# Memory layers in a periodic order with three of four chain images transposed by DMA

## The chip, the cores and the metric

The kernel runs on one core of one Trainium2 chip. A core has TensorE (matmuls into PSUM, a small memory of eight banks), VectorE, ScalarE and GpSimd for elementwise work, SyncE (SP), which here only issues DMAs, and 16 DMA engines. Every engine takes its instructions in the order written, and engines wait for one another through semaphores. The metric is the device time of one execution in microseconds. Three runs of the kernel before gave a median of 2031.8 us (2031.22 to 2032.16).

## The reference

Input x is 2048 rows of 512 numbers in bf16. Four layers follow one another, each adding its result to x: a memory layer A, a linear attention layer B, A again, B again. Each works on the layer-normalised x.

```python
for s in range(n_seg):                    # 64 segments of 32 rows
    h = concatenate([mem, xs])            # 8 memory rows + 32 rows of x
    q, k, v = h @ Wq, h @ Wk, h @ Wv      # 32 heads of 128
    scores = q @ k.T * scale              # 40 x 40, causal among the rows of x;
                                          # every query sees all 8 memory rows
    o = softmax(scores) @ v @ Wo
    mem = o[:8]                           # goes into the next segment
    outs.append(o[8:])
```

The 8 memory rows of a segment come out of the segment before, so layer A is a recurrence of 64 steps. Layer B is, for 32 heads of 16, o = phi(q) (phi(k)^T v) / (phi(q) sum phi(k)), then a projection; it has no recurrence over segments.

## The kernel before

A step of the recurrence uses a block of 32 rows: the 8 memory rows and 24 of the segment's 32 rows of x. The remaining 8 rows of each of four segments do not fit; they form a block of 32 "left" rows, one for each group of four segments (`left_block`, line 671), worked on ahead of time.

**Chain images.** `project` (line 633) multiplies a block by half of the heads of a weight matrix: 16 matmuls of 512 columns, each on one of four column tiles of the array, so that 32 rows of output stand at four places of PSUM. For queries and keys the result is copied to SBUF as an image of 128x512 and must then be transposed for the scores. `transposed` (line 645) does this on TensorE for the four images of a segment (queries and keys, each in two halves of the heads): four transposes into PSUM (L655) and a copy. `turned` (line 662) does it for the left block by one DMA transpose from SBUF to SBUF (L668), issued on SP. Values need no transpose.

**Memory attention** (line 708), for each half: a mask matmul (L717), scores of the memory's queries against left keys and own keys (L725), an exponential, sums (L737), a reciprocal by logarithm and exponential (L740, L742), products with the values (L750, L751), a multiplication (L754). Then comes the output projection (L823, column tiles) and `next_mem` (L842), which selects the 8 new memory rows and puts them into the next block: the recurrence closes there.

**x attention** (line 759) treats the other queries, off the recurrence: its scores (L774) are 32 matmuls on column tiles, for each head over 24 own queries and 8 left queries side by side. For this the left queries are copied behind the own ones into `qT` first, which is 40 wide for this purpose (line 768). Sums (L786, L787), products (L807, L808) and, a segment later, the output projection follow; `residual` (L857) adds the rows to x.

**Order.** `_Prog.schedule` (line 125) writes the order of all engines by a list scheduler over a table of costs. Among the instructions that are ready on an engine it picks the one with the highest priority, which is the length of the longest chain behind it (its "tail"). On TensorE it prefers an instruction of the same mode (column tiles, "col", or full array, "full") if its priority is within `MODE_SLACK`, and counts `PE_SWITCH` = 0.1 us for a change of mode. PSUM tiles take one of the eight banks when their first instruction is picked. Instructions marked urgent, those of the recurrence, may take one of the last free banks.

## Time and profile before

| | us |
|---|---|
| median of three runs | 2031.8 |
| profiled execution | 2032.45 |
| its span, first to last instruction | 2030.7 |
| TensorE busy | 1946.7 (96%) |
| ScalarE busy | 1274.8 (63%) |
| VectorE busy | 1015.3 (50%) |
| DMA transposes | 128, 2.5 from issue to landing |

In a row of the profile stand the line of the kernel, the engine (PE is TensorE's matmuls, PEld its weight loads, DVE VectorE, ACT ScalarE, SPq SP's queue), the operation, what is written and read, the shape and how many. In a group of instructions the busy time, the mean duration of one in ns and the idle time ahead of them follow; in a view in order of time the start and duration stand first. Durations of matmuls overlap, since they are pipelined: what a matmul costs is the time until the next one starts.

### The profile page before, as it was taken

What the parts mean: (1) busy time and instruction counts of PE and PEld (TensorE: products, weight loads), DVE (VectorE), ACT (ScalarE), POOL (GpSimd) and SP (SyncE); (2) the same over time, 40 slices, a digit from 0 to 9 for tenths busy, and PEclk for the clock granted to TensorE, in tenths of its full rate; (3) what the DMA queues carried; (4) which work ended last, traced back from release to release, by engine and by line L of the source; (5) the groups of instructions that cost most, each with busy time, mean ns of one, the idle gap of its engine ahead of it and who ended that gap; (6) DMA issues with size and microseconds to landing.
All of it is one profiled execution on the core that took longest, in us unless ns stands there. A gap on an engine that the chain in (4) does not pass through costs nothing.

```text
span 2030.7 us, 81374 instructions
## 1 busy us (share of the span) xinstructions
PE 1946.7 (96%) x37214; PEld 1150.5 (57%) x37214; DVE 1015.3 (50%) x3068; ACT 1274.8 (63%) x3203; POOL 23.6 (1%) x88
## 2 busy tenths in 40 slices
PE   2999999999999999997989999999999999999988
PEld 0555556555555555554645555555556555555555
DVE  0544444544444444445865444444444444444578
ACT  1666666666666666665646666666666666666654
POOL 3000000000000000000010000000000000000000
PEclk8999999999999999998999999999999999999989
DMA  9100000000000000001010000000000000000011
GB/s 362 34 10 13 10 13 11 12 10 13 13 11 13 13 14 10 13 8 43 1 15 16 8 13 11 13 13 13 10 13 13 10 11 13 13 10 13 5 42 43
DMA packets 82184, 47.17 MB, mean 23 GB/s; under 512 B 70056, under 2 KB 79280, under 8 KB 80304
## 3 DMA queue, kind: packets, MB, share of 16 engines
q1 hardware_dynamic: 81840, 41.97, 9.0%
q8 instruction: 291, 4.77, 1.0%
q14 instruction: 53, 0.43, 0.1%
HBM read 23.08 MB, written 2.10 MB: 12 GB/s over the span
## 4 chain that ended last, share of the span: by engine, by line
PE 93%; DMA 2%; DVE 2%; ACT 1%; issue 0%; SPq 0%; DVEq 0%
PE pb L639 43%; PE pb L823 15%; PE pb L655 6%; PE pb L842 3%; PE pb L807 3%; PE pb L944 3%; PE pb L725 3%; PE pb L857 2%; PE pb L737 2%; DMA Wv_sb<-in_A_Wv_dram 2%; PE pb L717 2%; PE pb L774 2%; PE pb L1011 1%; PE pb L937 1%; PE pb L750 1%; PE pb L751 1%
## 5 line engine op out<-in xcount | busy, mean ns | idle before, releaser
L516 ACT ACTIVATE arena_sb<-pb 128x512 bf16<-128x512 f32 (+6 forms) x1535 | 796.0, 523 | 421.9 <-PE pb L639 275.7
L639 PE MATMUL pb<-Wk_sb,arena_sb 128*32 128x512 bf16 x5120 | 353.3, 384 | 0.8 <-ACT arena_sb L516 0.8
L823 PE MATMUL pb<-Wo_sb,arena_sb 128*32 128x512 bf16 x5184 | 337.1, 384 | 8.7 <-DVE arena_sb L754 8.3
L639 PE MATMUL pb<-Wq_sb,arena_sb 128*32 128x512 bf16 x5120 | 344.4, 383 | 0.5 <-ACT arena_sb L516 0.5
L517 DVE COPY arena_sb<-pb 128x512 bf16<-128x512 bf16 (+2 forms) x474 | 178.5, 405 | 311.1 <-PE pb L655 307.4
L639 PE MATMUL pb<-Wv_sb,arena_sb 128*32 128x512 bf16 x5120 | 323.5, 380 | 0.5 <-DMA Wv_sb<-in_A_Wv_dram 0.5
L795 DVE TENSOR_TENSOR arena_sb<-arena_sb 32x256 bf16<-32x256 bf16 x512 | 213.3, 417 | 162.5 <-ACT arena_sb L791 150.6
L517 DVE CAST arena_sb<-pb 128x128 bf16<-128x128 f32 (+3 forms) x357 | 132.7, 375 | 179.6 <-PE pb L808 64.0
L639 PEld LDWEIGHTS pb<-Wk_sb,arena_sb 128*32 128x32 bf16 x5120 | 132.9, 97 | 126.9 <-issue 5.1
L639 PEld LDWEIGHTS pb<-Wq_sb,arena_sb 128*32 128x32 bf16 x5120 | 127.2, 97 | 130.7 <-ACT arena_sb L516 7.6
L639 PEld LDWEIGHTS pb<-Wv_sb,arena_sb 128*32 128x32 bf16 x5120 | 130.6, 96 | 121.7 <-DMA Wv_sb<-in_A_Wv_dram 0.6
L823 PEld LDWEIGHTS pb<-Wo_sb,arena_sb 128*32 128x32 bf16 x5184 | 122.1, 96 | 120.8 <-issue 11.3
L516 ACT ACTIVATE outW_sb<-pb 128x256 fp32r<-128x256 f32 x155 | 59.3, 382 | 184.8 <-PE pb L823 184.7
L655 PE MATMUL pb<-id_sb,arena_sb 128*128 128x128 bf16 x2048 | 157.3, 219 | 0.0
L655 PEld LDWEIGHTS pb<-id_sb,arena_sb 128*128 128x128 bf16 x2048 | 122.6, 97 | 55.4 <-ACT arena_sb L516 54.4
L807 PE MATMUL pb<-arena_sb 128*128 128x128 bf16 x1024 | 125.0, 217 | 4.1 <-DVE arena_sb L797 4.1
L797 DVE TENSOR_TENSOR arena_sb<-arena_sb 32x64 bf16<-32x64 bf16 x512 | 111.1, 217 | 15.8
L808 PE MATMUL pb<-arena_sb 128*128 128x32 bf16 x1024 | 114.3, 178 | 0.0
L732 ACT ACTIVATE arena_sb<-pb 128x256 bf16<-128x256 f32 x256 | 92.4, 383 | 32.9 <-PE pb L725 27.2
L842 PEld LDWEIGHTS pb<-selm_sb,outW_sb 128*128 128x128 f32 x504 | 75.1, 188 | 64.8 <-ACT arena_sb L778 23.8
L725 PE MATMUL pb<-arena_sb 128*128 128x32 bf16 x2048 | 102.8, 177 | 0.0
L517 DVE CAST outW_sb<-pb 128x256 fp32r<-128x256 f32 x105 | 44.5, 424 | 106.5 <-ACT outW_sb L516 103.4
(106 smaller groups left out, 2314.0 us busy)
## 6 DMA issues: line engine op xcount, KB each, us to landing
Wk_sb<-in_A_Wk_dram SPq DMA_DIRECT2D x1, 4096.0 KB, 12.6
Wq_sb<-in_A_Wq_dram SPq DMA_DIRECT2D x1, 4096.0 KB, 22.7
Wv_sb<-in_A_Wv_dram SPq DMA_DIRECT2D x1, 4096.0 KB, 31.9
Wo_sb<-in_A_Wo_dram SPq DMA_DIRECT2D x1, 4096.0 KB, 43.8
arena_sb<-in_B_wqkv_dram SPq DMA_DIRECT2D x2, 1536.0 KB, 6.3
arena_sb<-arena_sb SPq DMA_TRANSPOSE x128, 2.5
out_dram<-x_sb SPq DMA_DIRECT2D x16, 128.0 KB, 1.7
x_sb<-in_A_x_dram SPq DMA_DIRECT2D x1, 1920.0 KB, 9.3
```

The source lines that it names most:

```text
L516: return e.activation(o() if callable(o) else o, i() if callable(i) else i, ACTF.Copy)
L517: return e.tensor_copy(o() if callable(o) else o, i() if callable(i) else i)
L639: r = pe.matmul(tl.f32()[32 * j:32 * j + 32, 0:512], blk[:, c, :], W[:, c, o:o + 512], start=(c == 0), stop=(c == 3), tile_position=(0, 32 ...
L655: r = pe.transpose(tt.bf16()[:, 128 * i:128 * i + 128], img[:, k, 128 * i:128 * i + 128], id_sb[:, :])
L725: r = pe.matmul(tl.f32()[:, o:o + 32], kk[:, hh, :, :].rearrange("p j x -> p (j x)"), qT[:, r2, hh, :, 0:8], start=False, stop=True, skip_ ...
L732: add("act", lambda a: a.activation(Pm[:, k, :, :].rearrange("p a q -> p (a q)"), tl.f32()[:, 0:256], ACTF.Exp, scale=SCALE), c_act(256), ...
L795: add("dve", lambda v, q=q, j=j: v.tensor_tensor(Pbx[q, :, j, 0:32], Px[q, :, :], Rx[q, :, :], ALU.mult), c_dve(256), reads=["Px", "Rx"], ...
L797: add("dve", lambda v, q=q, j=j: v.tensor_tensor(Pbx[q, :, j, 32:40], PLL[q, g2, :, gl], Rx[q, :, 24:32], ALU.mult), c_dve(64), reads=[("P ...
L807: pe.matmul(o, vimg[:, r2, e], Pbx[:, hh, :, 0:32], start=True, stop=False)
L808: return pe.matmul(o[:, :, 24:32], vleft[:, g2, e], Pbx[:, hh, :, 32:40], start=False, stop=True)
L823: r = pe.matmul(tl.f32()[32 * j:32 * j + 32, :], oT[:, 4 * hh + j, :], Wo_sb[:, 8 * j + hh, :], start=(hh == 0), stop=(hh == 7), tile_posi ...
L842: r = pe.matmul(tl.f32()[:, 8 * c:8 * c + 8], outW[:, s % 3, 128 * c:128 * c + 128], selm_sb[:, :], start=True, stop=True)
```

## The change

The change has three parts.

First, `transposed` and `turned` become one function with a switch. Of a segment's four images, both halves of the queries and the first half of the keys now go through a DMA transpose on SP; the second half of the keys stays on TensorE. The scheduler's figures for a DMA transpose change from 0.1 us of issue and 3.0 us of latency to 1.25 and 1.25.

Second, the left queries are no longer copied into `qT`, which is 32 wide now. The x scores do, for each head, one matmul over the 24 own queries and one over the 8 left queries where they lie.

Third, the order. Each instruction of the memory layers gets a place: the segment (step), a kind of work and a number in it. Its priority is -(step x PERIOD + offset), from a table of offsets for each kind, in place of its tail. `MODE_SLACK` becomes 18.45. The rule by which the second of two matmuls into one tile took over the first one's priority is gone. New "soft" edges hold back the first instruction of a tile that is not urgent until the other inputs of that tile's later instructions have been made. Nodes without a place (the setup, layer B) keep their tail.

```diff
-MODE_SLACK = 2.0
+MODE_SLACK = 18.45
+PERIOD = 13.5
+OFFSET = {
...
+    "qk0": (-1.45, 4.35, 1.15, -14.55, 1.75, -4.85),
+    "qk1": (-0.85, -0.95, 2.70, 0.15, 0.50, -1.15, 4.25),
...
+    "mem0": (-7.70, -1.90, -2.45, 0.40, -1.90, -0.15, -0.35, 0.55, 2.20),
+    "mem1": (19.35, -0.45, 0.15, -2.40, -13.55, 0.30, 0.00, 0.00, 0.10),
...
+}
...
+        for nd in nodes:
+            for tl in nd.tiles:
+                if tl.ops[0] is nd and not nd.urgent:
+                    for op in tl.ops[1:]:
+                        nd.soft.update(d for d in op.sync if d.done is None and d.idx < nd.idx)
...
             nd.prio = nd.tail
-            for tl in nd.tiles:
-                k = tl.ops.index(nd)
-                if k and tl.ops[k - 1] in nd.order and tl.ops[k - 1].done is None:
-                    nd.prio = max(nd.prio, tl.ops[k - 1].prio)
+            if nd.key is not None and OFFSET:
+                step, name, k = nd.key
+                nd.prio = -(step * PERIOD + OFFSET[name][k])
...
+    QDMA = (True, True)
+    KDMA = (True, False)
...
-        def transposed(W, key, blk, bkeys, b, dst, dkey, urgent):
+        def turned(W, key, blk, bkeys, b, dst, dkey, urgent, dma):
...
+            if dma:
+                add("sp", lambda e: e.dma_start_transpose(dst.rearrange("p h j x -> p h (j x)"), img[:, k, :]), 1.25,
+                    reads=[("img", k)], writes=[dkey], dsem="turn%d" % k, lat=1.25)
+                return nd
...
-                add(ANY, copy(qT[:, r2, hs, :, 32:40], qTl[:, g2, hs, :, gl]),
-                    {"act": c_act(128, 0, 1), "dve": c_dve(128)}, reads=[("qTl", g2, b)], writes=[("qTL", r2, b)])
...
-                            r = pe.matmul(tl.f32()[32 * j:32 * j + 32, 32 * hh:32 * hh + 32], kT[:, r2, hh, j, :],
-                                          qT[:, r2, hh, j, 8:40], start=True, stop=True, tile_position=(0, 32 * j))
+                            q = slice(32 * j, 32 * j + 32)
+                            pe.matmul(tl.f32()[q, 32 * hh:32 * hh + 24], kT[:, r2, hh, j, :], qT[:, r2, hh, j, 8:32],
+                                      start=True, stop=True, tile_position=(0, 32 * j))
+                            r = pe.matmul(tl.f32()[q, 32 * hh + 24:32 * hh + 32], kT[:, r2, hh, j, :],
+                                          qTl[:, g2, hh, j, gl], start=True, stop=True, tile_position=(0, 32 * j))
...
-                transposed(Wq_sb, "Wq", blk, bk, b, qT[:, r2, hs, :, 0:32], ("qT", r2, b), True)
-                early.append(transposed(Wk_sb, "Wk", blk, bk, b, kT[:, r2, hs, :, :], ("kT", r2, b), True))
+                turned(Wq_sb, "Wq", blk, bk, b, qT[:, r2, hs, :, :], ("qT", r2, b), True, QDMA[b])
+                early.append(turned(Wk_sb, "Wk", blk, bk, b, kT[:, r2, hs, :, :], ("kT", r2, b), True, KDMA[b]))
```

More of the change, by code (lines that the diff above doesn't have):

```diff
@@ L56 @@
     __slots__ = ("engs", "fn", "cost", "sync", "order", "tiles", "dsem", "dval", "eng", "start", "done",
-                 "tail", "sig", "val", "waits", "know", "idx", "succ", "nleft", "urgent", "mode", "prio", "lat")
+                 "tail", "sig", "val", "waits", "know", "idx", "succ", "nleft", "urgent", "mode", "prio", "lat", "soft", "key")
 class _Prog:
@@ L73, in __init__, with at, again @@
         self.pe_mode = None
+        self.place = None
+        self.count = 0
+    def at(self, *place):
+        self.place = place or None
+        self.count = 0
+    def again(self):
+        self.count -= 1
     def tile(self):
@@ L82, in add @@
         nd.lat = lat
+        nd.key = None
+        if self.place is not None:
+            step, name = self.place
+            nd.key = (step, name, self.count)
+            self.count += 1
+        nd.soft = set()
         nd.engs = (engs,) if isinstance(engs, str) else tuple(engs)
@@ L135, in schedule @@
         for nd in nodes:
+            for tl in nd.tiles:
[3 more added lines that the diff above has]
+        for nd in nodes:
             nd.nleft = 0
-            for d in nd.sync | nd.order:
+            for d in nd.sync | nd.order | nd.soft:
                 if d.done is None:
@@ L144, in schedule @@
             for s in nd.succ:
+                if nd not in s.sync and nd not in s.order:
+                    continue
                 v = s.tail + (0.0 if nd in s.order else lag)
@@ L164, in rtime @@
                 t = max(t, d.done + lag)
-            for d in nd.order:
+            for d in nd.order | nd.soft:
                 t = max(t, d.done)
@@ L635, in project @@
             for c in range(4):
+                if c:
+                    P.again()
                 def mm(pe, c=c):
@@ L675, in left_block @@
             for b in range(2):
+                P.at(step, "left%d" % b)
                 hs = slice(4 * b, 4 * b + 4)
-                turned(Wq_sb, "Wq", blk, bk, b, qTl[:, r2, hs, :, :], ("qTl", r2, b))
-                turned(Wk_sb, "Wk", blk, bk, b, kTl[:, r2, hs, :, :], ("kTl", r2, b))
+                turned(Wq_sb, "Wq", blk, bk, b, qTl[:, r2, hs, :, :], ("qTl", r2, b), False, True)
+                turned(Wk_sb, "Wk", blk, bk, b, kTl[:, r2, hs, :, :], ("kTl", r2, b), False, True)
             for b in range(2):
+                P.at(step, "leftv%d" % b)
                 tl = project(Wv_sb, "Wv", blk, bk, b, False)
@@ L820, in out_proj @@
             for hh in range(8):
+                if hh % 4:
+                    P.again()
                 def mm(pe, hh=hh):
```

55 lines of the change are left out of this document (37 added, 18 removed).

## The prediction

> **What bounds the kernel now.** I read the page first, for the engines and the chain that ended last; then the busy times of a steady stretch of the first memory layer; then TensorE's instructions in order of time through one segment; then the DMA transposes; last the start.
>
> ```profile
> PE 1946.7 (96%) x37214; PEld 1150.5 (57%) x37214; DVE 1015.3 (50%) x3068; ACT 1274.8 (63%) x3203; POOL 23.6 (1%) x88
> ...
> PE 93%; DMA 2%; DVE 2%; ACT 1%; issue 0%; SPq 0%; DVEq 0%
> ```
>
> The chain that ended last is TensorE for 93% of the span, so what counts is time on TensorE's queue. The next two views are the busy times between 100 and 900 us (TensorE, its weight loads, VectorE, ScalarE, GpSimd, granted clock, DMA), and one of the groups of instructions there.
>
> ```profile
> 100.00:900.00 800.00, 795.67 (x15973) 468.13 (x15974) 383.59 (x1202) 525.81 (x1332) 0.00 (x0) 1.00 0.07 12
> ```
>
> ```profile
> L717 PE MATMUL pb<-arena_sb,u_sb 128*128 128x256 bf16 x114 | 31.2, 273 | 0.0
> ```
>
> TensorE is busy 795.67 of 800 us at the full granted clock (1.00). L717 runs twice a segment, so 114 of them are 57 segments, 800 / 57 = 14.04 us each. VectorE (383.59) and ScalarE (525.81) have room. A microsecond of TensorE's queue saved per segment is therefore worth 128 us in the two memory layers, as long as nothing makes the queue wait. The duration of one (273 ns) overlaps its neighbours'; costs have to be read from start to start:
>
> ```profile
> 174.00 1.04 PE L639 MATMUL pb<-Wk_sb,arena_sb 128*32 128x512 bf16 x16
> 174.86 1.04 PE L639 MATMUL pb<-Wq_sb,arena_sb 128*32 128x512 bf16 x16
> ...
> 178.42 0.62 PE L655 MATMUL pb<-id_sb,arena_sb 128*128 128x128 bf16 x8
> 178.88 0.27 PE L717 MATMUL pb<-arena_sb,u_sb 128*128 128x256 bf16 x1
> 178.99 0.61 PE L655 MATMUL pb<-id_sb,arena_sb 128*128 128x128 bf16 x8
> 179.43 0.26 PE L725 MATMUL pb<-arena_sb 128*128 128x32 bf16 x4
> 179.54 0.27 PE L717 MATMUL pb<-arena_sb,u_sb 128*128 128x256 bf16 x1
> 179.74 0.40 PE L639 MATMUL pb<-Wk_sb,arena_sb 128*32 128x512 bf16 x4
> 180.07 0.47 PE L725 MATMUL pb<-arena_sb 128*128 128x32 bf16 x12
> ...
> 180.98 0.18 PE L750 MATMUL pb<-arena_sb 128*128 128x32 bf16 x1
> 181.00 0.18 PE L751 MATMUL pb<-arena_sb 128*128 128x32 bf16 x1
> 181.03 0.18 PE L750 MATMUL pb<-arena_sb 128*128 128x32 bf16 x1
> ...
> 181.53 0.40 PE L639 MATMUL pb<-Wk_sb,arena_sb 128*32 128x512 bf16 x4
> ...
> 182.39 2.19 PE L823 MATMUL pb<-Wo_sb,arena_sb 128*32 128x512 bf16 x36
> 184.39 0.43 PE L774 MATMUL pb<-arena_sb 128*32 128x32 bf16 x32
> 184.65 0.84 PE L823 MATMUL pb<-Wo_sb,arena_sb 128*32 128x512 bf16 x12
> 185.42 0.39 PE L842 MATMUL pb<-selm_sb,outW_sb 128*128 128x8 f32 x2
> 185.74 0.40 PE L823 MATMUL pb<-Wo_sb,arena_sb 128*32 128x512 bf16 x4
> ```
>
> Here 128*32 marks a matmul on one of four column tiles, 128*128 one on the full array. Sixteen projection matmuls take 0.86 us (174.00 to 174.86), four 0.216.
>
> **The change, term by term, per segment.**
>
> **Transposes taken off TensorE.** The four chain images' transposes are L655, four matmuls each, here at 178.42 and 178.99. Three of the images (both query halves, the first key half) lose theirs. Eight take 178.42 to 178.88, so 57.5 ns each: 12 x 57.5 = **-0.69 us**, all on the path. The copies behind them leave VectorE and ScalarE, which were not the bound: nothing.
>
> **Left queries apart.** The x scores (L774, 32 matmuls of 32 columns) become 64: for each head 24 own queries and 8 left queries, one straight behind the other on the same column tile, each with its own weight load. Now 32 of them take 184.39 to 184.65, 0.26 us, 8 ns each, because four tiles take turns. The trace has no two neighbours on one column tile. The nearest rows are L750 and L751, 32 columns each on the whole array, 25 ns from start to start (180.98, 181.00, 181.03 after rounding). At the low end pairs overlap as well as now: 64 x 8 = 0.52, +0.26. At the high end nothing overlaps: 64 x 25 = 1.60, +1.34. I take 25 ns inside a pair, because both need the same tile as L750 and L751 need the same array, and an estimated 4 ns (half of 8) to the next tile, because that step changes tile as it does today: 32 x 29 = 0.93, **+0.67 us**. The two copies of left queries that disappear were VectorE's or ScalarE's: nothing. So the first two terms nearly cancel.
>
> On 8 columns costing as much as 32, the Trainium skill's TensorEngine Tiling (Array Packing), Instruction Overhead, says that a matmul has an overhead of about 60 cycles, that one column takes as long as 60, and that a factor should not be taken from a dimension that is already small. At the skill's 2.4 GHz that is an estimate of 25 ns; charged to all 64 one after the other it would make this term 1.6 - 0.26 = +1.34. The trace agrees on 25 ns for L750 and L751 and disagrees for column tiles that alternate (8 ns).
>
> **Fewer changes between column tiles and full array.** Four L639 between two full-array pieces take 179.74 to 180.07, 0.33 where 0.216 is their own: +0.11. The single L717 before them takes 0.20 (179.54 to 179.74) where the earlier one takes 0.11 (178.88 to 178.99): +0.09. A round trip costs 0.20 us, and the segment above has five (column work before 178.42, at 179.74, at 181.53, from 182.39 to 184.65, at 185.74). MODE_SLACK goes from 2.0 to 18.45 and now compares places in a 13.5 us period, so the scheduler stays in a mode while anything ready there is not over a period late. Two round trips are forced (projections, memory scores, output projection, next memory). The bounds are five (0) and two (-0.60); The soft edges, which hold back a tile's first matmul until the other inputs of that tile are there, and the places themselves only reorder, so they are priced here and not again. I take three, since waits for exponentials will still leave one hole: 2 x 0.20 = **-0.40 us**.
>
> **Waits for the transposes.** They go out on SP, in order, beside the left blocks' own.
>
> ```profile
> L668 SPq DMA_TRANSPOSE arena_sb<-arena_sb x14: 1189/1190/2152, 114.7 to 294.2; - x14
> ...
> DMA to landing us min/median/max: 2.4/2.5/4.4
> ```
>
> ```profile
> 175.09 0.60 ACT L516 ACTIVATE arena_sb<-pb 128x512 bf16<-128x512 f32 x1 [0.27 <-PE pb L639]
> ```
>
> One issue holds SP's queue 1.19 us; landing takes 2.4 to 2.5, at times 4.4. An image is copied from 0.23 us after its projection (174.86 to 175.09), for 0.60. Three projections in a row end at 0.86, 1.72 and 2.58 us; the first issue is possible at 0.86 + 0.83 = 1.69, the third at 1.69 + 2 x 1.19 = 4.07, and it lands at 6.5. Today the last block of memory scores starts at 180.07, 6.9 us after the projections that begin at 173.13 by the same rows (174.00 less 0.86). On time, the DMA path is thus 0.4 us early; 1.9 us late it is 1.5 behind. Late landings are common: counting all 120 from 114 us on, 48 took over 2.8 us, 3.8 on average. Two windows around one transpose each show why:
>
> ```profile
> q8 instruction: 1, 0.02, 1.9%
> issues: line engine op xcount, KB each, median us to landing
> arena_sb<-arena_sb SPq DMA_TRANSPOSE x1, 4.2
> ```
>
> ```profile
> q1 hardware_dynamic: 544, 0.13, 25.2%
> issues: line engine op xcount, KB each, median us to landing
> arena_sb<-arena_sb SPq DMA_TRANSPOSE x1, 2.4
> ```
>
> The late one shares its window with an instruction fetch (q8), the other does not. Behind the waiting scores stand, in TensorE's fixed order, the x attention's products and the output projection, so a late landing that no filler covers stops the engine. Lower bound 0 (the column work of left block and x scores, some 2 us a segment, lies in front); upper bound two waits a segment, 0.4 of them late by 3.8 - 2.45 = 1.35: 1.1. I take 0.4 x an estimated 0.5 left uncovered, because only the third image is tight: **+0.20 us**.
>
> **Start.** Nodes of the setup carry no place, so they keep their long tail as priority and pass all placed ones on SP; the load of the first memory is issued before the left transposes instead of behind one.
>
> ```profile
> 47.98 0.27 PE L597 MATMUL pb<-id_sb,arena_sb 8*128 8x8 bf16 x4 [11.73 <-DMA arena_sb<-in_A_mem_dram]
> ```
>
> ```profile
> Wo_sb<-in_A_Wo_dram SPq DMA_DIRECT2D x1, 4096.0 KB, 43.8
> ```
>
> TensorE waits 11.73 us for that load, until 47.98. Wo's load, ahead of it in the queue, needs 43.8 us from its issue near 3, so to about 47: **-1 us** once, between 0 and -2. The linear attention layers run the same instructions; only their order may move: nothing, bounds 2 us either way.
>
> **Sum.** -0.69 + 0.67 - 0.40 + 0.20 = -0.22 us; x 128 = -28; -1 at the start: -29. The profiled execution took 2032.45 (1.75 of it around the span of 2030.7); 2032.45 - 29 = **2003 us**. Its time is 0.65 over the median of 2031.8, too little to correct for.
>
> **Rivals.**
>
> A. *Pairs overlap as four tiles do now.* +0.26 in place of +0.67: 128 x -0.41 = -52, 1951 us. For it: 8 ns today with every weight load apart. Against: those neighbours are on different tiles.
>
> B. *Late landings pass through (slower).* Place: L725 waiting for a DMA in TensorE's queue; price 1.1 in place of 0.20, 128 x 0.9 = +115, 2118 us. It decides, turning the gain to a loss, from 0.20 + 29 / 128 = 0.43 us a segment. For it: 40% late, the third image only 0.4 us early. Against: 2 us of column filler that can stand in front.
>
> The Trainium skill's VectorE: DVE Perf Modes, The three transpose paths and its rules, speaks for this side: TensorE for a 128x128 transpose where PSUM will do, 390 ns against 1309 ns by DMA. An estimate by its figures is 4 x 1.309 = 5.2 us an image and 20.9 us for four a segment, which would make the queue the bound at 128 x 6.9 = 880 us more. The trace disagrees: a whole image lands in 2.5 us and the next may be issued after 1.19, so it gets no chance here.
>
> C. *Nothing overlaps in the pairs.* All 64 at 25 ns: +1.34 in place of +0.67, +86, 2089 us. Against: weight loads run ahead today. The Trainium skill's TensorEngine Tiling (Array Packing), Instruction Overhead, read for every matmul alone, gives this.
>
> D. *The new order does not do what it says.* Round trips stay at five: +0.40, +51, 2054 us. For it: VectorE's and ScalarE's steps between TensorE's pieces are unchanged. Against: the constant in the scheduler is nine times larger.
>
> **How the numbers follow.** Forecast 0.45, A 0.20, B 0.16, C 0.09, D 0.10. The forecast's own range, with two to four round trips and 0 to 0.4 us of waiting, is 1977 to 2032. The range reaches from a little below A to C: 1945 to 2090, leaving out most of B. A measurement of this kernel can tell about 0.2%, 4 us, from no change. Faster: A, 0.38 of the forecast's 0.45, 0.01 of D: 0.59. Within 0.2%: 0.05 of the forecast and 0.01 of D: 0.06. The rest, 0.35, is slower.
>
> **What would show it.** L655 at 512 instead of 2048 and 512 DMA transposes; L774's successor with 64 matmuls a segment spanning 0.93 us start to start (0.5: A; 1.6: C); three column stretches a segment (five: D); idle of the weight loads before the L725 successor put down to the DMA, 26 us in total at 0.20 a segment, above 55 for B; the first memory's transposes before 48 us. I am wrong if the period between L717 pairs is not near 13.8 us.

## The result, and the profile after

The changed kernel takes 1981.5 us, the median of four runs (1977.7 to 1983.7), against 2031.9 for the kernel before on the same chip: a ratio of 0.975, with a 95% interval of 0.973 to 0.977. That is 50 us less. The forecast was 2003 us, so faster was right and the size was 22 us short.

The page of the changed kernel, its lines on the engines' busy times, on the chain that ended last and on the groups that bear on this case:

```profile
PE 1844.6 (93%) x39774; PEld 1116.5 (56%) x39774; DVE 845.2 (43%) x2453; ACT 1259.0 (64%) x3178; POOL 23.7 (1%) x88
...
PE 78%; DMA 18%; ACT 2%; DVE 1%; SPq 1%; issue 0%
...
L774 PE MATMUL pb<-arena_sb 128*128 128x32 bf16 x2048 | 99.3, 177 | 47.0 <-DMA arena_sb<-arena_sb 45.4
...
arena_sb<-arena_sb SPq DMA_TRANSPOSE x512, 2.5
```

TensorE is still the bound, but no longer alone: it held 93% of the chain and holds 78% now, and 18% are DMAs. The memory scores (L774, before L725) stood idle for nothing before; now 45.4 us of idle time on TensorE are put down to the transposes' landings. DMA transposes went from 128 to 512, and TensorE is busy 102 us less. Busy times between 100 and 900 us (TensorE, its weight loads, VectorE, ScalarE, GpSimd, granted clock, DMA), and who waited for the DMA transposes in the whole span (us, times; PEld are the weight loads):

```profile
100.00:900.00 800.00, 772.38 (x17679) 469.83 (x17675) 316.87 (x950) 537.29 (x1370) 0.00 (x0) 1.00 0.24 41
```

```profile
  PEld pb L774: 65.4, 105
  PE pb L774: 45.4, 86
  PE pb L735: 13.0, 12
```

TensorE idles 27.6 of these 800 us, where it idled 4.3. The waits are at the memory scores (L774) and, in a few places, at the left queries' scores (L735): (45.4 + 13.0) / 128 = 0.46 us a segment. The weight loads at L774, which come ahead of the matmuls, idle for longer, 65.4 us, since the matmuls before still count as busy while the queue waits.

How long a segment takes is read from the selection of the new memory, which comes once a segment. One row of each kernel holds the whole first layer: the first matmul and the last of 63 selections, four each. The kernel before, then the changed one:

```profile
L842 PE MATMUL pb<-selm_sb,outW_sb x252: 167/253/273, 63.6 to 923.7; 128*128 128x8 f32 x126
```

```profile
L900 PE MATMUL pb<-selm_sb,outW_sb x252: 252/253/273, 67.5 to 899.4; 128*128 128x8 f32 x126
```

The period falls from (923.7 - 63.6) / 62 = 13.87 us to (899.4 - 67.5) / 62 = 13.42. In the second memory layer, taken from the same instructions, it falls from 13.85 to 13.43. So 62 x (0.45 + 0.42) = 54 us come off in the two layers. The first selection comes 3.9 us later, at 67.5, which takes part of that back; the stretches between and behind the memory layers grow by about 1 us together. That accounts for the 49 us between the two profiled executions (2032.45 and 1983.74): the whole result is the period, less the start.

TensorE's instructions in order of time through one segment of the changed kernel (start and duration first, idle time and its releaser in brackets):

```profile
600.58 0.27 PE L774 MATMUL pb<-arena_sb 128*128 128x32 bf16 x4 [0.64 <-DMA arena_sb<-arena_sb]
...
602.05 0.18 PE L800 MATMUL pb<-arena_sb 128*128 128x32 bf16 x1
602.16 0.21 PE L821 MATMUL pb<-arena_sb 128*32 128x24 bf16 x4
602.20 0.19 PE L823 MATMUL pb<-arena_sb 128*32 128x8 bf16 x4
602.22 0.19 PE L821 MATMUL pb<-arena_sb 128*32 128x24 bf16 x4
602.25 0.19 PE L823 MATMUL pb<-arena_sb 128*32 128x8 bf16 x4
602.27 0.19 PE L821 MATMUL pb<-arena_sb 128*32 128x24 bf16 x4
...
602.63 0.20 PE L823 MATMUL pb<-arena_sb 128*32 128x8 bf16 x3
602.67 2.79 PE L878 MATMUL pb<-Wo_sb,arena_sb 128*32 128x512 bf16 x48
605.39 0.61 PE L900 MATMUL pb<-selm_sb,outW_sb 128*128 128x8 f32 x4
605.86 0.28 PE L835 MATMUL pb<-arena_sb,bo_sb 128*128 128x256 bf16 x1
605.98 0.19 PE L836 MATMUL pb<-arena_sb,bo_sb 128*128 128x64 bf16 x1
606.10 0.61 PE L878 MATMUL pb<-Wo_sb,arena_sb 128*32 128x512 bf16 x8
606.55 1.04 PE L688 MATMUL pb<-Wk_sb,arena_sb 128*32 128x512 bf16 x16
...
611.29 1.04 PE L688 MATMUL pb<-Wv_sb,arena_sb 128*32 128x512 bf16 x16
612.26 0.28 PE L766 MATMUL pb<-arena_sb,u_sb 128*128 128x256 bf16 x1
612.81 0.36 PE L774 MATMUL pb<-arena_sb 128*128 128x32 bf16 x8 [0.26 <-DMA arena_sb<-arena_sb]
613.02 0.38 PE L708 MATMUL pb<-id_sb,arena_sb 128*128 128x128 bf16 x4
```

Three things are to be seen in the rows. There are two stretches on column tiles (128*32) in the segment, from 602.16 and from 606.10, where the segment shown of before had five. The second key image is the only one still transposed here (L708, four matmuls). And the memory scores wait for a DMA twice, 0.64 and 0.26 us, and nothing else on TensorE waits.

### The profile page after: what moved, and what is told of

Its sections match the earlier page's. It is cut to its first block, busy times and chain, and to the rows that moved or that the text cites. A ratio compares the mean times of both kernels' runs of the same rounds, so it can differ in the third digit from the quotient of the medians.

```text
span 1981.8 us, 86163 instructions
## 1 busy us (share of the span) xinstructions
PE 1844.6 (93%) x39774; PEld 1116.5 (56%) x39774; DVE 845.2 (43%) x2453; ACT 1259.0 (64%) x3178; POOL 23.7 (1%) x88
## 4 chain that ended last, share of the span: by engine, by line
PE 78%; DMA 18%; ACT 2%; DVE 1%; SPq 1%; issue 0%
PE pb L688 33%; DMA arena_sb<-arena_sb 16%; PE pb L878 15%; PE pb L1007 3%; PE pb L900 3%; PE pb L774 3%; PE pb L821 3%; PE pb L859 3%; PE pb L916 2%; DMA arena_sb<-in_A_mem_dram 2%; PE pb L786 2%; PE pb L1000 1%; PE pb L1074 1%; ACT arena_sb L562 1%; PE pb L800 1%; PE pb L799 1%
## 5 line engine op out<-in xcount | busy, mean ns | idle before, releaser
L562 ACT ACTIVATE arena_sb<-pb 128x512 bf16<-128x512 f32 (+6 forms) x1507 | 748.3, 505 | 334.0 <-PE pb L688 204.5
L688 PE MATMUL pb<-Wk_sb,arena_sb 128*32 128x512 bf16 x5120 | 336.8, 381 | 0.5 <-ACT arena_sb L562 0.5
L688 PE MATMUL pb<-Wq_sb,arena_sb 128*32 128x512 bf16 x5120 | 325.3, 382 | 0.8 <-ACT arena_sb L562 0.8
L878 PE MATMUL pb<-Wo_sb,arena_sb 128*32 128x512 bf16 x5184 | 321.1, 383 | 0.5 <-ACT arena_sb L562 0.5
L563 DVE COPY arena_sb<-pb 128x512 bf16<-128x512 bf16 (+2 forms) x200 | 72.5, 363 | 496.4 <-PE pb L708 426.5
L562 ACT ACTIVATE outW_sb<-pb 128x256 fp32r<-128x256 f32 x226 | 86.8, 384 | 173.3 <-PE pb L878 170.2
L878 PEld LDWEIGHTS pb<-Wo_sb,arena_sb 128*32 128x32 bf16 x5184 | 140.2, 96 | 100.2 <-DVE arena_sb L803 9.8
L563 DVE CAST arena_sb<-pb 128x128 bf16<-128x128 f32 (+2 forms) x275 | 118.7, 432 | 118.4 <-ACT arena_sb L562 58.3
L774 PE MATMUL pb<-arena_sb 128*128 128x32 bf16 x2048 | 99.3, 177 | 47.0 <-DMA arena_sb<-arena_sb 45.4
L774 PEld LDWEIGHTS pb<-arena_sb 128*128 128x128 bf16 x2048 | 79.4, 96 | 69.2 <-DMA arena_sb<-arena_sb 65.4
L846 DVE TENSOR_TENSOR arena_sb<-arena_sb 32x64 bf16<-32x64 bf16 x512 | 111.0, 217 | 15.8
L859 PEld LDWEIGHTS pb<-arena_sb 128*128 128x128 bf16 x1024 | 91.2, 96 | 3.3 <-DVE arena_sb L846 3.3
L803 DVE TENSOR_TENSOR arena_sb<-pb,arena_sb 128x128 bf16<-128x128 f32 x256 | 74.2, 290 | 40.5 <-ACT arena_sb L791 31.2
```

The source lines that it names most:

```text
L562: return e.activation(o() if callable(o) else o, i() if callable(i) else i, ACTF.Copy)
L563: return e.tensor_copy(o() if callable(o) else o, i() if callable(i) else i)
L688: r = pe.matmul(tl.f32()[32 * j:32 * j + 32, 0:512], blk[:, c, :], W[:, c, o:o + 512], start=(c == 0), stop=(c == 3), tile_position=(0, 32 ...
L774: r = pe.matmul(tl.f32()[:, o:o + 32], kk[:, hh, :, :].rearrange("p j x -> p (j x)"), qT[:, r2, hh, :, 0:8], start=False, stop=True, skip_ ...
L803: add("dve", lambda v: v.tensor_tensor(oTb[:, s % 3, 16 * b:16 * b + 16, 0:8], pv.f32()[:, 0:128].rearrange("p (n q) -> p n q", q=8), Rm[: ...
L846: add("dve", lambda v, q=q, j=j: v.tensor_tensor(Pbx[q, :, j, 32:40], PLL[q, g2, :, gl], Rx[q, :, 24:32], ALU.mult), c_dve(64), reads=[("P ...
```

## Experiments

### Each part alone

Either half of the change can be made without the other. The first kernel takes the DMA transposes and the separate left queries into the kernel before, with its scheduler as it was:

```diff
+    QDMA = (True, True)
+    KDMA = (True, False)
...
+            if dma:
+                add("sp", lambda e: e.dma_start_transpose(dst.rearrange("p h j x -> p h (j x)"), img[:, k, :]), 1.25,
+                    reads=[("img", k)], writes=[dkey], dsem="turn%d" % k, lat=1.25)
+                return nd
...
-                                           qT[:, r2, hh, j, 8:40], start=True, stop=True, tile_position=(0, 32 * j))
+                            pe.matmul(tl.f32()[q, 32 * hh:32 * hh + 24], kT[:, r2, hh, j, :], qT[:, r2, hh, j, 8:32],
+                                      start=True, stop=True, tile_position=(0, 32 * j))
```

> The changed kernel's data path (three images by DMA, left queries apart) with the scheduler of before (tails as priorities, MODE_SLACK 2.0, no places, no soft edges). Theory 1 (sum of terms): per segment -0.69 for the transposes, +0.25 for the 64 x scores at the 0.5 us that the changed kernel's profile shows, waits for late landings of 0.2 to 0.5, and round trips still near 4.9: between -0.24 and +0.06 us, so 2000 to 2040 us. Rival (the gain is the transposes' and the order only accompanies them): near 1982 us as the changed kernel.

Measured: 2090.1 us, 1.029 of before (1.028 to 1.031). The page's lines on the chain and on the scores:

```profile
PE 74%; DMA 17%; DVE 4%; ACT 3%; issue 1%; SPq 1%; DVEq 0%; ACTq 0%
...
L770 PE MATMUL pb<-arena_sb 128*128 128x32 bf16 x2048 | 111.2, 178 | 64.1 <-DMA arena_sb<-arena_sb 61.9
```

The scores wait 61.9 us for landings, and the trace has 5.5 changes from column tiles to the full array per segment, more than before (4.8, counted over 50 segments). Less work on TensorE, and 59 us slower, outside what either expectation said. In the old scheduler's order the landings are not covered, and the modes change more often.

The second kernel takes the new order, with its places, slack and soft edges, onto the data path of before. The places of the extra transposes and copies, which the table has not got, are mine: each follows the image it belongs to.

```diff
-MODE_SLACK = 2.0
+MODE_SLACK = 18.45
+PERIOD = 13.5
+OFFSET = {...}
...
+    QDMA = (False, False)
+    KDMA = (False, False)
```

> The new order (places, soft edges, MODE_SLACK 18.45) on the data path of before: all four images transposed on TensorE, left queries copied, x scores as 32 matmuls. The four images' transposes and copies have offsets like those of the second key half. Theory 1: round trips fall from 4.9 to about 2.2 a segment at 0.2 us each, -0.53 us, no DMA waits in the recurrence: 2032 - 68 + 4 (later start) = 1968 us, no slower than the changed kernel. Rival (the order only pays because DMA takes the transposes out of the way): 2015 to 2035 us.

Measured: 2076.8 us, 1.022 (1.021 to 1.024). The chain of waits, by engine:

```profile
PE 72%; DVE 13%; ACT 10%; DMA 2%; issue 2%; SPq 1%; DVEq 0%
```

The changes of mode fall to 3.5 a segment, but VectorE and ScalarE, at 2% and 1% of the chain before, now hold 13% and 10%. Most of VectorE's part are the x attention's multiplications by the reciprocals (L846 and L848, 9.7% of the span); on ScalarE the copies out of PSUM come first (L562, 4.1%). Neither expectation held, since the time is above both. Alone the halves cost 59 and 46 us, together they gain 50. They are not terms that can be added. How much of the second loss is the order itself and how much my unfitted places stays open.

### What groups the column work

```diff
-MODE_SLACK = 18.45
+MODE_SLACK = 2.0
```

> The changed kernel with MODE_SLACK back at 2.0, places kept. Theory 1 (the slack is what keeps TensorE in one mode): round trips rise from 2.2 towards 4.9 a segment, +0.2 to +0.5 us, 2007 to 2045 us. Rival (the table of offsets does the grouping by itself): round trips stay near 2.2 and the time within 10 us of 1981.5.

Measured: 2117.8 us, 1.042 (1.039 to 1.045), with 5.9 changes of mode a segment instead of 2.0. The page on the scores:

```profile
L774 PE MATMUL pb<-arena_sb 128*128 128x32 bf16 x2048 | 95.5, 177 | 71.0 <-DMA arena_sb<-arena_sb 69.4
```

It is the slack that groups the column work, as the prediction had it, and the table of places does not do it by itself. The time rises by 136 us, 1.06 a segment: 3.9 changes x 0.20 are 0.78 of that, and the scores wait longer, 69.4 for 45.4 us or 0.19 a segment. No run takes the soft edges or the places away by themselves, so what they add to the slack is open.

### The second matmul of the x scores

The order of every instruction stays that of the changed kernel; each pair becomes one matmul, which leaves out the scores of the left queries.

```diff
-                            pe.matmul(tl.f32()[q, 32 * hh:32 * hh + 24], kT[:, r2, hh, j, :], qT[:, r2, hh, j, 8:32], ...)
-                            r = pe.matmul(tl.f32()[q, 32 * hh + 24:32 * hh + 32], kT[:, r2, hh, j, :], qTl[:, g2, hh, j, gl], ...)
+                            r = pe.matmul(tl.f32()[q, 32 * hh:32 * hh + 32], kT[:, r2, hh, j, :], qT[:, r2, hh, j, 0:32], ...)
```

> The changed kernel with the x scores as 32 matmuls of 32 columns over the block's first 32 queries; left out are the x scores of the left queries (and 8 memory queries are scored in place of the last own ones). Theory 1 (x scores lie on TensorE's path and cost twice 0.26 us): 0.26 us a segment less, 1981.5 - 33 = 1949 us. Rival (pairs on one column tile run one after the other, as the prediction had it): -0.67, 1896 us. Rival 2 (waits for landings take up what is saved): 1975 to 1983 us.

Measured: 1958.1 us, 0.964 (0.962 to 0.966), 23.4 us less than the changed kernel or 0.18 a segment. The trace shows 0.25 of TensorE's queue saved (64 matmuls in the 0.51 us from 602.16 to 602.67, eight ns each, against 32); where the other 0.07 went, no row shows. The forecast's term of 0.67 us would have been 86 us here, and is out. No run keeps the copies of the left queries in the new order, so whether the second part of the change pays by itself is open.

The two memory layers of this one execution differ, and that is a measurement by itself. The rows of the scores' waits in the first layer and in the second:

```profile
L774 PE MATMUL pb<-arena_sb x1016: 176/176/191, 63.5 to 906.7; 128*128 128x32 bf16 x170
its engine sat idle before it (us, times) until:
  DMA arena_sb<-arena_sb: 27.0, 45
```

```profile
L774 PE MATMUL pb<-arena_sb x1024: 176/176/190, 1025.8 to 1852.0; 128*128 128x32 bf16 x171
its engine sat idle before it (us, times) until:
  DMA arena_sb<-arena_sb: 15.7, 30
```

Two passes over the same work in the same order of segments: 27.0 us of waiting in one layer and 15.7 in the other, with periods of 13.40 and 13.10 us. In the first layer 39% of the transposes landed late (over 2.8 us), in the second 30%. Against the changed kernel (13.42 and 13.43) the first layer thus saved 0.02 us a segment and the second 0.33, and the 0.18 is their mean. The waits make up 11 of the 19 us between the two layers; that the number of late landings moves a layer this far is the likely reading, with 8 us left open.

### What the waits for landings cost

To price the waits, the memory scores read the images of the segment before, which have landed long ago. The order of every engine and all the work stay: the plan still holds the scores behind the new images, and that edge is dropped when the semaphores are written.

```diff
+            nd.sync -= nd.loose
...
+            ro = r2 if s == 0 else 1 - r2
-                                  qT[:, r2, hh, :, 0:8], start=False, stop=True, skip_group_check=True)
+                                  qT[:, ro, hh, :, 0:8], start=False, stop=True, skip_group_check=True)
...
-            add("pe", lambda pe: mm(pe, 0, kT[:, r2, :, :, :]), ...)
+            add("pe", lambda pe: mm(pe, 0, kT[:, ro, :, :, :]), ...)
```

> The changed kernel in exactly its planned order, but the memory scores read the queries and keys of the segment before, which landed long ago, and do not wait for this segment's transposes (all DMAs still run; left out is thus the use of the right queries and keys in the memory scores). Theory 1 (the waits for landings before the memory scores, 0.5 us a segment, are lost time on TensorE's queue): 1981.5 - 0.5 x 128 = 1917 us, at best 1900. Rival (another wait of the recurrence stands right behind and takes most of it back): 1950 us or more.

Measured: 1920.3 us, 0.945 (0.943 to 0.946), 61.2 us less than the changed kernel: 61.2 / 128 = 0.48 us a segment. The page's chain and the scores' row, and the row of the selections:

```profile
PE 89%; DMA 6%; ACT 2%; DVE 1%; SPq 1%; issue 1%
...
L779 PE MATMUL pb<-arena_sb 128*128 128x32 bf16 x2048 | 97.7, 176 | 0.2 <-DMA arena_sb<-arena_sb 0.2
```

```profile
L908 PE MATMUL pb<-selm_sb,outW_sb x252: 252/253/273, 67.8 to 870.7; 128*128 128x8 f32 x126
```

The idle time at the scores is gone (0.2 us for 45.4), the period is (870.7 - 67.8) / 62 = 12.95, 0.47 less, and the chain is TensorE's again. This is shown, not argued: the memory scores' waits for landings take back 61 us of what the change saves. That is close to the 65.4 us by the weight loads and more than the 45.4 by the matmuls. The share of DMAs in the chain (18%, some 350 us) is far more than they cost, since the chain counts the whole time of a transpose from its issue. The left scores' waits are still there (15.6 us on TensorE in this kernel, 13.0 in the changed one).

### What the transposes cost

The one image left on TensorE is transposed four times over, 12 matmuls more a segment, as many as the change took away.

```diff
-                for i in range(4):
+                for i in [0, 1, 2, 3] * 4:
```

> The changed kernel in exactly its planned order; the one image that stays on TensorE is transposed four times over, so TensorE has the 16 transposes a segment of the kernel before at the place of the changed kernel's four (and the DMA transposes too). Theory 1 (what was taken off TensorE lies wholly on its path): 12 x 0.056 = 0.67 us a segment, 1981.5 + 86 = 2068 us. Rival (part of it would be hidden by waits that are there anyway): 2010 to 2045 us.

Measured: 2046.3 us, 1.007 (1.005 to 1.008), 64.8 us or 0.51 a segment above the changed kernel. The order of time around one such group, and the scores' row of the page:

```profile
608.89 1.05 PE L708 MATMUL pb<-id_sb,arena_sb 128*128 128x128 bf16 x16
609.78 0.22 PE L859 MATMUL pb<-arena_sb 128*128 128x128 bf16 x1
```

```profile
L774 PE MATMUL pb<-arena_sb 128*128 128x32 bf16 x2048 | 98.6, 177 | 38.6 <-DMA arena_sb<-arena_sb 37.6
```

Sixteen take 0.89 us, so twelve take 0.67, as the forecast had it (0.69). Of these 0.67 the end feels 0.51, three quarters, and the x scores gave the same: 0.18 of 0.25. A part of this shows: the scores wait 37.6 us instead of 45.4. Taken apart by the image that a matmul waits for (waits over 0.1 us), those of the first half keep their 35 us and those of the second half fall from 11.2 to 3.4. L708 stands between the two in 117 of the 128 segments: work ahead of a wait shortens it. That is 8 us of the 21 missing, 14 by the weight loads (51.7 for 65.4); for the rest I have no row.

### How many images by DMA

Two of the chain images by DMA in place of three (the second half of the queries goes back to TensorE), and then all four; the places of the nodes that come or go are mine again.

```diff
-    QDMA = (True, True)
+    QDMA = (True, False)
```

> The changed kernel with the second query half back on TensorE, so two images by DMA and two on TensorE. Theory 1 (the third image in SP's queue is the tight one, as the prediction had it): +0.23 us of transposes, waits before the memory scores fall from 0.5 to 0.15, net -0.12 x 128 = -15 us, 1966 us. Rival (each of the images is as likely to be late and to stop the queue): +0.23 - 0.17, 1989 us, or more where the places no longer fit.

```diff
-    KDMA = (True, False)
+    KDMA = (True, True)
```

> The changed kernel with the second key half by DMA too, four images a segment. Theory 1: -0.23 us of transposes, a fourth place in SP's queue lands 1.19 us later, at about 7.7 us after the projections begin, and waits rise by 0.4 or more: 1995 us or more. Rival (DMA transposes are hidden, every one taken off TensorE is a gain): 1981.5 - 29 = 1952 us.

Measured: with two 2031.1 us, 1.000 (0.999 to 1.001), with 3.0 changes of mode; with four 2468.8 us, 1.216 (1.212 to 1.220). The scores' row of the kernel with two:

```profile
L774 PE MATMUL pb<-arena_sb 128*128 128x32 bf16 x2048 | 106.2, 177 | 46.5 <-DMA arena_sb<-arena_sb 46.1
```

With the third image gone from SP's queue the scores wait as long as before (46.1 for 45.4 us), all of it ahead of the first half's scores: the theory that only the third image is tight fell, as far as this replanned order shows. The chain of the kernel with four and its busy times between 100 and 900 us (TensorE, weight loads, VectorE, ScalarE, GpSimd, clock, DMA):

```profile
PE 65%; DVE 12%; DMA 12%; ACT 8%; issue 2%; SPq 0%; DVEq 0%
```

```profile
100.00:900.00 800.00, 694.88 (x13541) 375.24 (x13541) 207.30 (x635) 439.74 (x1127) 0.00 (x0) 0.89 0.24 40
```

With four TensorE is busy 694.9 of 800 us at a granted clock of 0.89, where the changed kernel has 772.4 at 1.00, and VectorE and ScalarE hold a fifth of the chain, with 4.0 changes of mode a segment: the order has come apart. How much of the loss is the lower clock is not separated. DMA landings are 12% of that chain, less than in the changed kernel, and the DMA engines are as busy in the same stretch (0.24 in both), so the rows do not put the 487 us on the traffic of the fourth transfer. Both kernels are in line with the halves: the table fits one plan.

### The latency that the plan assumes

One figure of the scheduler: transposes are planned to land 1.5 us later, 4.0 us behind their issue, where the late ones take 3.65 on the mean.

```diff
-                    reads=[("img", k)], writes=[dkey], dsem="turn%d" % k, lat=1.25)
+                    reads=[("img", k)], writes=[dkey], dsem="turn%d" % k, lat=2.75)
```

> The changed kernel; only the scheduler's figure for a transpose's latency behind its issue goes from 1.25 to 2.75 us (all transposes), so it plans for landings of 4.0 us instead of 2.5. Nothing else is edited; the order follows. Theory 1 (late landings stop TensorE because the plan leaves no slack): the waits before the memory scores fall from 0.5 to 0.2 us a segment or less and the time by 0.3 x 128 = 38 us, to about 1943 us. Rival (the places are fitted to the short latency, and a longer recurrence in the plan makes the order worse): 1990 us or more, with more round trips than 2.0.

Measured: 2214.3 us, 1.091 (1.089 to 1.093). The chain and the scores' waits:

```profile
PE 81%; DVE 6%; ACT 6%; DMA 4%; issue 2%; SPq 1%; DVEq 0%
```

```profile
L774 PE MATMUL pb<-arena_sb x2048: 176/176/207, 62.1 to 2109.7; 128*128 128x32 bf16 x187
its engine sat idle before it (us, times) until:
  DMA arena_sb<-arena_sb: 5.5, 9
```

My theory that a plan with room for late landings is faster fell. The room is there, the scores wait 5.5 us instead of 45.4, and yet the time is 233 us longer: the changes of mode go to 5.4 a segment and the period to 15.3 us. Waiting has moved from the landings to VectorE and ScalarE, 6% of the chain each.

### The start

The first selection came 3.9 us later than before, although the forecast had 1 us earlier. VectorE's first work on x, and the first transposes of the memory rows, in the changed kernel:

```profile
33.92 0.69 DVE L656 BATCH_NORM_STATS2 st_sb<-x_sb 128x6 f32<-128x512 bf16 x1 [15.30 <-DMA x_sb<-in_A_x_dram]
...
46.19 0.25 PE L643 MATMUL pb<-id_sb,arena_sb 8*128 8x8 bf16 x4 [4.08 <-DMA arena_sb<-in_A_mem_dram]
```

```profile
24.36 0.69 DVE L610 BATCH_NORM_STATS2 st_sb<-x_sb 128x6 f32<-128x512 bf16 x1 [21.16 <-DMA x_sb<-in_A_x_dram]
```

The last row is the kernel before. The memory's transposes do come earlier, at 46.19 for 47.98, as forecast. But the first rows of x now go out behind the third weight matrix instead of ahead of it, and are there at 33.9 instead of 24.4 us. Three kernels moved the start. The first gives the loads of x and the memory priority in the planner, which then also plans the rest anew:

```diff
+            if nd.dsem in ("dx0", "dmem"):
+                nd.prio = 1e6
+            if nd.dsem == "dx1":
+                nd.prio = -5.0
```

> The changed kernel with the loads at the start reordered: the first 128 rows of x and the first memory ahead of the weights, the other rows of x behind the first segment's transposes. Theory 1 (the start is bound by when the first memory and the first x land, behind 16 MB of weights): the first new memory, now at 67.5 us, comes 8 to 15 us earlier and the time is 1967 to 1974 us. Rival (the first transposes queue behind the weights anyway and set the start): within 4 us of 1981.5.

Measured: 1977.2 us, 0.974 (0.973 to 0.975). The first selection comes at 58.7 us, 8.8 earlier, and only 4.3 us are seen at the end, less than the 8 to 15 expected. The other two leave the order of the changed kernel on every engine but SP, and reorder SP's loads alone: the first five row tiles of x and the memory ahead of the weights, the rest of x behind seven transposes.

```diff
...
+        self.committed = [x0, mem] + rest[:at] + [wo, x1] + rest[at:]
...
```

> The changed kernel with the order of every engine but SP exactly as it stands there; on SP alone the rows of x for the first five row tiles (640 KB in one load) and the first memory go out ahead of the weights, and Wo's load and the rest of x go out behind the first seven transposes. The same work is done. Theory (the start is a fixed loss in front of the recurrence, and what it loses comes off the end one for one as long as the order is that of the changed kernel): the first selection of new memory rows, at 67.5 us in the changed kernel, comes at 52 to 59 us; the period stays at 13.41 to 13.43 us; the time falls by as much as the first selection moves, to 1968 to 1973 us. Rival (the period depends on how the setup leaves the queues, as when the start was changed together with the planner's order: the first selection came 8.8 us earlier and the time fell by 4.3): the period rises by 0.04 us or more and the time is 1976 us or above.

```diff
-        self.committed = [x0, mem] + rest[:at] + [wo, x1] + rest[at:]
+        self.committed = [x0, mem] + rest[:at] + [x1] + rest[at:]
```

> As the run before it (the changed kernel's order on every engine but SP; x's first five row tiles and the first memory ahead of the weights, the rest of x behind the first seven transposes), but with Wo's load left where the changed kernel has it, behind Wv's. In the run before, the first output projection waited 13.9 us for Wo's load, the first selection of new memory rows came at 77.5 us, 10.0 us later than in the changed kernel, and the time rose by 9.7 us. Theory (a loss ahead of the recurrence comes off the end one for one while the order stays): Wo has landed by 50 us, nothing waits for it, the first selection comes at 55 to 63 us, the period stays at 13.40 to 13.44 us, and the time falls by as much as the first selection moves, to 1969 to 1977 us. Rival (an earlier start is given back later in the layers, only a later one is felt): the first selection comes as early, and the time stays within 2 us of 1981.5.

Measured: 1991.3 us, 0.980 (0.978 to 0.981), and 1977.8 us, 0.973 (0.972 to 0.975). The first of them was a miss. SP's queue and the output projection's first matmul there:

```profile
55.93 0.58 SPq L596 DMA_DIRECT2D Wo_sb<-in_A_Wo_dram  x1
...
70.52 1.90 PE L897 MATMUL pb<-Wo_sb,arena_sb 128*32 128x512 bf16 x16 [13.87 <-DMA Wo_sb<-in_A_Wo_dram]
```

I had put Wo's load behind the seven transposes as well, so it was issued at 55.93 and the output projection waited 13.87 us for it. The first selection came at 77.5 us, 10.0 later than in the changed kernel, and the time rose by 9.7: a loss ahead of the recurrence goes to the end one for one. With Wo's load back in its place the first selection comes at 60.9 us, 6.6 earlier, and the time is 3.7 lower. Its four runs (1974.9 to 1981.6) overlap those of the changed kernel, though, and in the profiled one the first layer had a period of 13.50, which is (13.50 - 13.42) x 62 = 5 us more. So a later start is shown to cost its length. An earlier one came out 4 us faster in both tries, less than it came forward, but the intervals of both ratios overlap that of the changed kernel (0.973 to 0.977), and with runs that spread over 6 us I can't say whether the rest is given back or only covered by chance. All three kernels move x and the memory together, so the share of x's first rows in the 3.9 us is not separated.

## Why the prediction was right, and where it was not

**The bound and the sign: right, the time in part by luck.** What counted was time on TensorE's queue per segment, and the waits in that queue. The forecast's own range, 1977 to 2032, holds the time because errors of both signs met: pairs and modes came out 0.58 us a segment cheaper than forecast, waits and start dearer. That range also moved one term at a time; two changes of mode with no waits and four with 0.4 us of them would have made it 1952 to 2054.

**Its own signs.** The period came to 13.42 us, where the prediction called itself wrong if it was not near 13.8. Part of that is a count: 800 us do not hold a whole number of segments, the period before was 13.87 and not 14.04, and the forecast's terms then give 13.65. The idle time of the weight loads ahead of the scores, 65.4 us, is above the 55 that was set as the sign of rival B. The other signs came as forecast or better: 512 transposes each way, 64 matmuls in 0.51 us (the sign of rival A), two stretches of column work, the first memory's transposes at 46.19 us.

| term, us a segment | forecast | measured | from |
|---|---|---|---|
| transposes off TensorE | -0.69 | -0.67 | sixteen L708 in 0.89 us |
| left queries apart | +0.67 | +0.25 | 64 in 0.51 us, 0.26 before |
| changes of mode | -0.40 | -0.56 | 4.76 to 1.98, at 0.20 |
| waits, memory scores | +0.20 | +0.48 | the kernel without them |
| waits, left scores | 0 | +0.10 | 13.0 us idle at L735 |
| sum | -0.22 | -0.40 | |
| period | | -0.45, -0.42 | the two layers |
| start, once | -1 | +3.9 | first selection |

The sum of what was measured is 0.02 to 0.05 us a segment, at most 6 us in all, short of the change of the period. With transposes and pairs at what the end felt of them (0.51 and 0.18) it would be -0.31, so the terms account for the period to about 0.1 us. The price of a change of mode holds in the changed kernel: the first full-array matmul behind a projection or the output projection starts a median of 0.12 us later than the next four column matmuls would, and the step back costs 0.08 (L800 to L821, 602.05 to 602.16, where L800 takes 0.025 otherwise).

**Transposes off TensorE: right,** with the price of the forecast.

**Left queries apart: the term that failed.** I took 25 ns inside a pair "because both need the same tile" and let the next tile's first matmul wait for the pair. The first half stands, the second fell. The code emits L821 and L823 alternately, the pair of one tile and then that of the next; the rows at 602.16 show four L821 starting first, which by the code are those of the four tiles, and then four L823. A group of four starts every 25 ns (602.20, 602.22, 602.25, 602.27), so a tile takes one of its own matmuls in that time, and the other three do the same beside it: eight in 0.05 us. In the second half of the 64 the two lines mix one by one, at 9 ns each on average (602.37 to 602.67). Rival A, which let pairs overlap as four tiles do now, had the price of 8 ns exactly; it got a chance of 0.20 and would have given 1951 us, which the waits then kept from happening. Rival C is out. The Trainium skill says in TensorEngine Tiling (Array Packing), Tiling Modes, Key Properties, that different tiles can load weights and multiply in parallel; the trace agrees, 64 in 0.51 us, and I should have weighed that sentence along with the one on overhead. It also says in TensorE: Matmul & The Clock Gate, Part 3: Packing small matmuls, that matmuls start and end strictly in program order; the rows at 602.16 to 602.27 do not agree for starts on different column tiles.

**Changes of mode: right in kind, short by one.** I took three because "waits for exponentials will still leave one hole". None was left: the trace counts 1.98. That the slack does it is shown by the kernel with a slack of 2.0, with 5.9. Rival D is out.

**Waits: right in place, mis-sized, and put on the wrong image.** They stand at L774, where rival B put them, with L735, the left scores, as a second place that the forecast did not have. I took 0.4 late landings a segment, each with 0.5 us left uncovered, "because only the third image is tight". The share of late ones was right (36% of 492 in the changed kernel, 3.65 us on the mean against 2.48). The 0.5 us was not: 0.4 x 1.35 = 0.54 is one image's late landings wholly uncovered, and 0.48 was measured. The reason was not either. In all 128 segments SP issues the first half's keys, then its queries, then the second half's queries. Of the waits over 0.1 us at the memory scores 35.3 us, in 60 places, are for the first half's queries, second in the queue, and 11.2 us, in 34, for the third image. In the rows shown the column work, 606.10 to 612.26, stands ahead of the mask (L766), and between the mask and the scores of the first half nothing is left to fill. That the grouping took the cover away is not shown: the kernels with the old slack and the old order group less and wait longer (69.4 and 61.9 us). The plan with the later landings shows that cover can be had, and that this table then loses more elsewhere. With 0.48 against the 0.43 from which rival B turns the forecast's gain to a loss, this term alone would have done so: 2003 + 128 x 0.28 = 2039 us. The pairs, 0.42 cheaper, and the modes, 0.16 cheaper, made up for it, and that is the luck.

**Start: wrong.** I followed the memory's load past the left transposes, since the trace of before showed that wait, and left out the other load in the same queue: x's first rows went behind Wv, and VectorE got them 9.6 us later. The step was right for its own load and said nothing of what was late next.

## What to carry to other kernels

An order found by search belongs to the plan that it was found on: a transfer moved, a latency or a slack changed in that plan cost 50 to 490 us here, while the same order with cheaper or dearer matmuls in it moved by about three quarters of their price (as the mean of two layers in one case). Half a change may lose where the whole gains, so price the order and the data path together. Small matmuls on column tiles were priced here tile by tile, at 25 ns on each of four tiles side by side, and not by the order in which they are written. And look which transfer a wait is for before you take one off the queue: here it was the second and not the last.

## What the hardware showed that was not expected

Matmuls on column tiles start out of program order: written as pairs, L821 then L823 on each tile in turn, they start as four L821 and then four L823 (602.16, 602.20), from then on a group every 25 ns through the first 32. That every engine takes its instructions in the order written thus does not hold for these starts.

Late landings of DMA transposes go with instruction fetches. Of the changed kernel's 492 transposes behind 100 us, 31% had a packet of the instruction queues in flight 1.15 to 2.15 us after their issue; 97% of these landed late, and 8% of the others. Most of the packets are of 16 KB (311 of 375 in the whole trace). The same count over the other thirteen traces gives 94 to 99% and 1 to 10%. It is a coincidence in time; no kernel moved the fetches, so that they are the cause, as the prediction took it, is not shown.

The granted clock fell to 0.89 in the kernel with four DMA images, whose TensorE was busy less (694.9 of 800 us) than in any other, and to 0.97 in the next, the one that plans for late landings (744.0). Why is open.
